# Attention placed by estimated due times, weight sums moved earlier, and a staggered last down product in a fused attention and maxout kernel

## Chip, cores and metric

The kernel runs on one core of one Trainium2 chip. The metric is the device time of one execution in microseconds (us): 328.72 us is the median of the three runs of the kernel before (327.97 the lowest).

## What is computed

The reference is attention followed by a feed-forward part that takes the largest of three up products:

```python
# q, k, v: batch 8, heads 12, tokens 448, head size 64
scores = scale * q @ k.T
m = max(scores); e = exp(scores - m)
attn = e / (sum(e) + exp(-m) + 1e-09)      # "softmax off by one"
x = (attn @ v), heads side by side         # 3584 tokens x 768
h = maximum(maximum(x @ w1, x @ w2), x @ w3)   # w1, w2, w3: 768 x 768
out = h @ w_out                            # 768 x 768, float32 out
```

## The kernel before

**Units of work.** Four heads of one batch make a group; there are 24 groups, three to a batch. A group's attention is cut into: seven score tiles ("U", `visit`, L306), each four matmuls on 64x64 quarters of TensorE into a pair of PSUM banks, followed by one `exp` on ScalarE (L317, 128x896); six sums of the exponentials on VectorE (`sum_e`, L327); the denominator ("D", `den_group`, L349: four matmuls with ones, then a logarithm on ScalarE, L362); its reciprocal as exp of minus that logarithm (`recip_group`, L369); and the product with v ("N", `num_group`, L373: 28 matmuls), whose two banks VectorE multiplies by the reciprocal into `xT` (`norm_group`, L397, two instructions). The feed-forward part is cut into pieces of 24 matmuls on 64x64 quarters (L789): an up piece (`up_piece`, evicted at L518, L520 or L523) or a down piece (`out_piece`, evicted at L567 or L575 and stored by `store`, L590).

**Three stages.** Up to about 74 us the first groups run with full 128x128 pieces (L534, L557). From there to 264 us every group's attention is laid among the pieces. The feed-forward part of the last two batches is done behind it, from 264 us on, with seven products in place of eight on half-size blocks (`up_unit` for the three up weights, `out_unit` for the down weight). This needs sums of weight blocks (`combine_weight`, L898, tiles `comb`), of x blocks (`combine_moving`, L907, tiles `sx`) and of h blocks (`sh`).

**What orders the middle stage.** The schedule is written out when the program is built; on the chip every engine runs its list in that order. `step` (L830) emits one step, a quarter-array matmul pair for each half of the rows, counted in `steps[0]`; a step stands for about 0.19 us of TensorE. `ORDER` (L858) is the order of a group, U U D U U N U U U, with the share of the group's steps that follow each part (`steps_for`). U, D and N take two pairs of PSUM banks in turn (`double`, L85), so that each one waits for what reads the banks of the one before the last: an exp, the logarithm, or the two norm multiplies. Work that must come some steps later is put in `late` by `after(n, ...)` and emitted by `do_late` (L801): the sums after 9, 14, 20 or 9 steps, and the two norm multiplies one and two steps after N. `given` holds, in steps, until when VectorE and ScalarE are booked; `give` and `first_free` add costs to it, and `first_free` uses it to choose the engine that evicts a piece.

**The last stage.** `in_turn` (L1134) emits the seven products of three units, product by product; a unit keeps two PSUM banks, "a" and "s", from a ring of eight (`tps`, L966, one pool with one tag, of which the first two turns are skipped). `put` (L1004) evicts a product's result; for weights 2 and 3 it goes to a buffer `c`, and `largest` (L1012) takes the maximum of all of `c` into `hp`, the tile `hT` of the last two batches, in one instruction of 1792 elements to a unit. `later(i)` puts the four sums for weight i+1 into slots 2 to 5 of weight i. After weight 3 the two held down tiles run (`plain`, L1107), then the four h sums, then the three units of `out_unit`: d[0] and d[1] side by side, d[2] mixed with the last plain tile at the end (L1153 to L1161). The output tiles of the units, `o1` and `o2`, come from the pool that the plain tiles use too (`out_pool`, five buffers). `ENDS` (L1056) gives the queues of the two stores of a tile: SP and SP, but POOL and POOL for `o2` of units 1 and 2.

Of the kernel before, what the change touches and what calls it, by code (L numbers as in the profile page):

```python
# [22 lines left out]
def kernel(  # L23
# [165 lines left out]

    steps = [0]  # L190
    given = {"dve": 0.0, "act": 0.0}

    def give(engine, cost):
        given[engine] = max(given[engine], steps[0]) + cost

    def first_free(dve_cost, act_cost):
        end = {e: max(given[e], steps[0]) + c for e, c in (("dve", dve_cost), ("act", act_cost))}
        e = "act" if end["act"] < end["dve"] else "dve"
        given[e] = end[e]
        return e  # L200

    def copy_qk(i, n):
        give("dve", 2.1)
# [102 lines left out]
    def visit(units):  # L306
# [8 lines left out]
        for st, j, stp in stps:  # L315
            give("act", 4.9)
            nc.scalar.activation(  # L317
                out=st["eT"][:, j], in_=stp[:, :, 0:S], func=AF.Exp, scale=scale, bias=-math.log(EDIV)
            )
        return mm  # L320

    def sum_e(i, j):
        give("dve", 3.3)
        st = state[i]
        if j == 1:
# [23 lines left out]
    def den_group(i):  # L349
# [10 lines left out]
        given["act"] = max(given["act"], given["dve"] + 2)  # L360
        give("act", 4.9)
# [4 lines left out]
    def recip_group(i):  # L366
        give("act", 5.1)
        st = state[i]
        nc.scalar.activation(  # L369
# [24 lines left out]
    def norm_group(i, banks, r):  # L394
        give("dve", 3.3)
# [108 lines left out]
    def up_piece(b, fc, i, bank=None, done=False):  # L504
# [12 lines left out]
        if i == 0 and done and first_free(3.3, 2.9) == "act":  # L517
# [3 lines left out]
        else:  # L521
            give("dve", 3.3)
# [28 lines left out]
    def out_piece(bp, t, nh, bank=None, done=False):  # L551
# [14 lines left out]
        if last or not done or first_free(2.9, 2.6) == "dve":  # L566
# [233 lines left out]

    def do_late(all_of=None):  # L801
        now = [x for x in late if x[0] <= steps[0] or x[1] is all_of]
        late[:] = [x for x in late if x not in now]
        for t, f, a in now:
            f(*a)
# [24 lines left out]
    def step():  # L830
        if count[0] == NDC * len(turns[0]) and (len(pieces) >= 3 or last_batch[0] and pieces):
# [4 lines left out]
            for r in range(2):  # L836
                turns[r] += [m + x for x in ((0, 2, 1), (1, 0, 2))[r] if x < len(now)]
        idle = not ready(0)
# [5 lines left out]
        do_late()  # L844

    def after(n, f, *a):
        late.append((steps[0] + n, f, a))

    debt = [0.0]

# [41 lines left out]
    def combine_weight(i, n):  # L892
        give("dve", 4.5)
# [19 lines left out]
    given.update(dve=0.0, act=0.0)  # L913
    batch_done(1)
    after(9, sum_e, MID, 1)
# [4 lines left out]
    for i in range(MID, NI + 1):  # L920
        for op, j, w in ORDER if i > MID else ORDER[4:]:
            if op == "U" and i < NI:
                mm = visit([(i, j)])
# [6 lines left out]
                if i == NI - 2 and j in (1, 3, 4, 6):  # L930
                    after(4, combine_weight, 0, (1, 3, 4, 6).index(j))
                if i == NI - 1 and j == 5:
                    after(4, lambda: combine_moving(sx, 2, *x_blocks()))
                if j > 0:
                    after({1: 9, 2: 14, 3: 20, 4: 9, 5: 9, 6: 9}[j], sum_e, i, j)
# [4 lines left out]
            if op == "D":  # L940
                if i == NI:
                    steps_for(12)
                do_late(sum_e)
                den_group(i - 1)
# [3 lines left out]
            if op == "N":  # L948
                pair = num_group(i - 1)
                steps[0] += 7  # L950
                for r in range(2):
                    after(1 + r, norm_group, i - 1, pair, r)
                b, g = groups[i - 1]
                if g == NG - 1:
                    after(10, batch_done, b)
            steps_for(rate[0] * w / TOTAL if i < NI else (8 if op == "D" else 0))
    while late or left() or count[1] < count[0]:
        step()

# [6 lines left out]
    tps = ctx.enter_context(tc.tile_pool(name="tps", bufs=8, space=bass.MemoryType.PSUM))  # L966
    for i in range(1, 4):
        comb[i] = tail.tile([128, 4, 3, DFF // 2], MMDT, name=f"comb{i}")
    for _ in range(2):
        tps.tile([128, 512], FP32, tag="tbank", name="first_two")  # L970
# [24 lines left out]
    def bank_of(u, which):  # L995
        u[which] = tps.tile([128, 512], FP32, tag="tbank", name="bank_" + which)

    def up_unit(i, f):
# [5 lines left out]
        def put(b, side, bank, other=None):  # L1004
# [4 lines left out]
            else:  # L1009
                nc.vector.tensor_tensor(out=dst, in0=other, in1=bank, op=ALU.add)  # L1010

        def largest():  # L1012
            if i > 0:
# [179 lines left out]
```

## Time and profile before

| | before |
|---|---|
| median of the runs | 328.72 us |
| the profiled execution, its own time | 329.01 us |
| its span, first to last instruction | 327.2 us |
| PE busy in the span | 304.5 us (93%) |
| DVE / ACT / POOL busy | 233.4 / 230.1 / 99.7 us |
| middle stage, first L789 matmul to last | 74.0 to about 263.3 us |
| first matmul of the last stage | 264.12 us |
| last matmul ends | 316.5 us |
| last work of DVE and ACT ends | 318.7 and 319.3 us |

Busy time says little here on PE: matmuls overlap (one of 448 columns is shown as 349 ns long, while four on different quarters start within 0.19 us), and a short pause of their starts can hide under the last one's end. So the holes are read from the starts in the timeline: where a run of L789 matmuls, which start about 0.05 us apart, is followed by a start that is late by more than that. The time outside the span is 1.8 us.

### The profile page before, as it was taken

To read this page: it belongs to the slowest core of one execution; us is meant where nothing else is said; L and a number is where in the kernel's file an instruction comes from. 1 tells how busy PE (TensorE), PEld (TensorE's weight loads), DVE (VectorE), ACT (ScalarE), POOL (GpSimd) and SP (SyncE) were. 2 spreads that over 40 slices of the span, in tenths; PEclk is the share of its full clock that TensorE was granted. 3 is DMA by queue.
4 is the path that set the end of the run, shared out by engine and by line. 5 is a ranking of instruction groups with operands and counts; after the bars stand their busy time and mean duration, and the time that the engine had idled before them with its cause. 6 is when DMAs were issued, how large, how long until landed. Compare 5 with 4: busy or idle time off the path is not lost.

```text
span 327.2 us, 12698 instructions
## 1 busy us (share of the span) xinstructions
PE 304.5 (93%) x5599; PEld 231.6 (71%) x5599; DVE 233.4 (71%) x426; ACT 230.1 (70%) x310; POOL 99.7 (30%) x171
## 2 busy tenths in 40 slices
PE   7679999999999999999999999899999999999960
PEld 6557777657777777889978899588976755555630
DVE  3437598997787777777868678788898475798720
ACT  2599859987776788788867897689777555464520
POOL 8767666640333233232323333232000000000020
PEclk9799999999999999999999999999999999999995
DMA  7999999999699997799977999969400150000365
GB/s 141 143 177 191 199 207 194 150 177 158 80 95 117 171 168 120 117 133 209 121 115 112 191 197 126 120 82 240 77 2 4 50 148 0 0 2 0 96 194 144
DMA packets 59352, 40.64 MB, mean 124 GB/s; under 512 B 32705, under 2 KB 55953, under 8 KB 59297
## 3 DMA queue, kind: packets, MB, share of 16 engines
q0 software_dynamic: 25584, 21.90, 47.8%
q1 hardware_dynamic: 33408, 17.50, 26.8%
q8 instruction: 44, 0.72, 0.9%
q10 hardware_dynamic: 304, 0.43, 0.5%
q14 instruction: 12, 0.09, 0.1%
HBM read 42.47 MB, written 11.01 MB: 163 GB/s over the span
## 4 chain that ended last, share of the span: by engine, by line
PE 77%; ACT 7%; issue 5%; DVE 5%; DMA 2%; POOL 2%; POOLq 0%; DVEq 0%
PE piece L789 37%; PE stp L293 8%; PE av L341 8%; PE bank_a L985 7%; PE bank_s L985 5%; PE p_i L534 4%; ACT eTp L416 3%; ACT eT L317 2%; PE piece L534 2%; DMA ld_q<-in_q_dram 2%; PE den L341 2%; DVE eS L327 2%; DVE hT L523 1%; DVE xT L397 1%; PE piece L557 1%
## 5 line engine op out<-in xcount | busy, mean ns | idle before, releaser
L317 ACT ACTIVATE eT<-stp 128x896 f16<-128x896 f32 x147 | 132.2, 917 | 40.7 <-PE stp L293 39.5
L789 PE MATMUL piece<-xT,w 64*64 64x448 f16 x2160 | 135.0, 349 | 0.5 <-DVE xT L397 0.3
L789 PEld LDWEIGHTS <-w 64*64 64x64 f16 x2160 | 90.0, 107 | 17.9 <-issue 2.0
L293 PE MATMUL stp<-qkT 64*64 64x448 f16 (+2 forms) x756 | 66.8, 334 | 3.3 <-DVE xT L397 1.0
L327 DVE TENSOR_TENSOR eS<-eS,eT 128x896 f16<-128x896 f16 x105 | 65.0, 619 | 3.7 <-ACT eT L317 1.1
L789 PE MATMUL piece<-w,hT 64*64 64x384 f16 x792 | 50.0, 323 | 0.3 <-DVE hT L523 0.2
L523 DVE TENSOR_TENSOR hT<-hT,piece 128x448 f16<-128x448 f16 x60 | 37.1, 619 | 18.4 <-PE piece L789 15.5
L112 POOL DMA_DIRECT2D ld_q<-in_q_dram x48 | 28.8, 606 | 53.2 <-PE stp L293 25.4
L112 POOL DMA_DIRECT2D ld_v<-in_v_dram x48 | 28.5, 599 | 46.9 <-PE stp L293 25.5
L789 PEld LDWEIGHTS <-hT 64*64 64x64 f16 x792 | 34.8, 107 | 4.8 <-issue 0.8
L293 PEld LDWEIGHTS <-qkT 64*64 64x64 f16 x756 | 28.5, 107 | 12.4 <-issue 6.7
L112 POOL DMA_DIRECT2D ld_k<-in_k_dram x46 | 27.9, 612 | 23.4 <-PE piece L789 10.6
L341 PE MATMUL av<-eT,ld_v 64*64 64x448 f16 x588 | 32.7, 349 | 0.0
L397 DVE TENSOR_TENSOR xT<-av,rb 128x448 f16<-128x448 f32 x42 | 24.2, 618 | 10.5 <-PE av L341 10.2
L341 PEld LDWEIGHTS <-ld_v 64*64 64x64 f16 x756 | 27.0, 108 | 5.4 <-issue 0.2
L590 POOL DMA_DIRECT2D out_dram<-o_sb x5 | 2.7, 538 | 91.6 <-DVE o_sb L1073 86.2
L416 ACT ACTIVATE eTp<-stp 128x768 f16<-128x768 f32 (+3 forms) x24 | 18.1, 821 | 9.4 <-PE stp L293 9.3
L534 PEld LDWEIGHTS <-w 128*128 128x128 f16 x216 | 18.9, 98 | 5.2 <-issue 3.9
L362 ACT ACTIVATE rb<-den 128x896 f32<-128x896 f32 x21 | 19.3, 918 | 3.9 <-PE den L341 3.3
L369 ACT ACTIVATE rb<-rb 128x896 f32<-128x896 f32 x21 | 20.0, 953 | 0.2
L567 DVE TENSOR_SCALAR o_sb<-piece 128x384 f32<-128x384 f32 x22 | 12.0, 554 | 9.1 <-PE piece L789 8.8
L985 PEld LDWEIGHTS <-comb 128*128 128x128 f16 x108 | 10.6, 98 | 9.9
(102 smaller groups left out, 335.1 us busy)
## 6 DMA issues: line engine op xcount, KB each, us to landing
out_dram<-o_sb SPq DMA_DIRECT2D x50, 192.0 KB, 4.0
ld_q<-in_q_dram POOLq DMA_DIRECT2D x48, 112.0 KB, 4.4
ld_v<-in_v_dram POOLq DMA_DIRECT2D x48, 112.0 KB, 4.1
ld_k<-in_k_dram POOLq DMA_DIRECT2D x46, 112.0 KB, 4.1
w<-in_moe_w_dram POOLq DMA_DIRECT2D x6, 192.0 KB, 6.7
w<-in_moe_w_out_dram POOLq DMA_DIRECT2D x3, 384.0 KB, 8.4
w<-in_moe_w_dram POOLq DMA_DIRECT2D x2, 384.0 KB, 6.2
out_dram<-o_sb POOLq DMA_DIRECT2D x4, 192.0 KB, 4.6
```

The lines of the kernel that those rows point to most:

```text
L112: return eng.dma_start(out=dst[hp * KC : hp * KC + KC].rearrange("p s j d -> p s (j d)"), in_=src[:, half_heads(name, hp)],)
L293: mm = nc.tensor.matmul(out=out[half(c), r], lhsT=qkT[half(r), 0, j, h], rhs=qkT[half(r), 1, q0:q1, h], start=True, stop=True,)
L317: nc.scalar.activation(out=st["eT"][:, j], in_=stp[:, :, 0:S], func=AF.Exp, scale=scale, bias=-math.log(EDIV))
L327: nc.vector.tensor_tensor(out=st["eS"], in0=st["eT"][:, 0] if j == 1 else st["eS"], in1=st["eT"][:, j], op=ALU.add,)
L341: nc.tensor.matmul(out=outs[r][half(c)], lhsT=weights(r, c), rhs=moving(r, c), start=start, stop=stop,)
L369: nc.scalar.activation(out=st["rb"], in_=st["rb"], func=AF.Exp, bias=math.log(LAMBDA), scale=-1.0)
L397: nc.vector.tensor_tensor(out=xT[b][:, 2 * g + r, :], in0=banks[r][:, 0:S], in1=state[i]["rb"][:, r], op=ALU.mult)
L416: nc.scalar.activation(out=eT[:, j0 : j0 + n].rearrange("p j r q -> p r j q"), in_=stp[:, :, 0 : n * nq].rearrange("p r (j q) -> p r j q", ...
L523: nc.vector.tensor_tensor(out=dst, in0=dst, in1=p_i[:, 0:S], op=ALU.max)
L534: nc.tensor.matmul(out=p_i[:, ts(j, nq)], lhsT=w_sb[i][:, dc, ts(2 * fp + j, 128)], rhs=xT[b][:, dc, q0 * KC : q1 * KC], start=(dc == 0), ...
L789: nc.tensor.matmul(out=p["bank"][half(c), 0:w], lhsT=lhs(k, r, c), rhs=rhs(k, r), start=(r == p["first"] and k == 0), stop=(r != p["first" ...
L985: nc.tensor.matmul(out=bank, lhsT=lhs(k), rhs=rhs(k), start=start and k == 0, stop=k == 2, skip_group_check=True,)
```

## The change

The kernel's first stage stays. In the middle stage:

- Costs in `given` are lowered (exp 4.9 to 4.2 steps, sums 3.3 to 2.8, and so on); `give` becomes `book`, which takes the time at which the data is ready and returns the booked end plus `SEEN` (1 step).
- `pair_free` keeps, for each pair of banks, the step at which it is estimated to be free. `for_pair` emits piece steps until then ahead of every U, D and N; those steps are taken off what `steps_for` emits later.
- A sum is due at the estimated end of its exp. D comes when its sums are booked as done. The two norm multiplies are emitted together (`norm_both`), due at the booked end of the reciprocal or one step after N.
- The four sums of weight 1 and the x sum `sx[2]` are no longer tied to units of the last two groups but lie in `spare`, from which `do_late` takes one whenever VectorE is booked as free; so weight 1's sums come at the start of the stage.

In the last stage:

- The eight banks come from four pools of 2, 4, 1 and 1 banks, used in the order 4, 2, 1, 1.
- The sums of weights 2 to 4 are moved forward by the table `LATER`: all of weight 2's and 3's lie in weight 1's slots (two in each of the last three), all of weight 4's in weight 2's, none in weight 3's.
- For weight 3, the maximum is taken by each `put` at once (448 elements each), and the last product's bank goes straight into the maximum on VectorE, in place of a ScalarE copy and one maximum of 1792 elements.
- `o1` and `o2` have buffers of their own, three each. Every store of the units goes half to SP, half to POOL.
- The h sums come after the first of the two held tiles; the second one's halves are used between the units' products; the three units are staggered instead of side by side.

```diff
+    def book(engine, cost, ready=0.0):
+        given[engine] = max(given[engine], ready, steps[0]) + cost
+        return given[engine] + SEEN
...
+            st["e", j] = pair_free[turn[0] % 2] = book("act", 4.2, steps[0] + 2)
...
+        st["sum"] = book("dve", 2.8, st["e", j])
...
+        pair_free[turn[0] % 2] = book("act", 4.3, steps[0] + 2)
...
+        if spare and given["dve"] <= steps[0]:
+            f, a = spare.pop(0)
             f(*a)
...
+    def steps_until(when):
+        while steps[0] < when():
+            debt[0] -= 1
+            if not step():
+                break
+    def next_pair():
+        return pair_free[(turn[0] + 1) % 2]
+    def for_pair(also=0.0):
+        steps_until(lambda: max(next_pair(), also))
+        if any(x[1] is norm_both and x[2][2] == (turn[0] + 1) % 2 for x in late):
+            do_late(norm_both)
...
+    def norm_both(i, pair, n):
+        for r in range(2):
+            norm_group(i, pair, r)
+        pair_free[n] = given["dve"] + SEEN
...
+        if i == NI - 2:
+            spare.append((combine_moving, (sx, 2, *x_blocks())))
...
+    spare += [(combine_weight, (0, n)) for n in range(4)]
...
             if op == "U" and i < NI:
+                for_pair()
                 mm = visit([(i, j)])
...
-                    after({1: 9, 2: 14, 3: 20, 4: 9, 5: 9, 6: 9}[j], sum_e, i, j)
+                    at(state[i]["e", j], sum_e, i, j)
...
             if op == "D":
-                if i == NI:
-                    steps_for(12)
+                steps_until(lambda: steps[0] + 1 if any(x[1] is sum_e for x in late) else 0)
                 do_late(sum_e)
+                for_pair(state[i - 1]["sum"])
                 den_group(i - 1)
...
             if op == "N":
+                for_pair()
                 pair = num_group(i - 1)
...
-                for r in range(2):
-                    after(1 + r, norm_group, i - 1, pair, r)
+                t = max(steps[0] + 1, state[i - 1]["recip"])
+                pair_free[n] = max(t, given["dve"]) + 5.6 + SEEN
+                at(t, norm_both, i - 1, pair, n)
...
-    tps = ctx.enter_context(tc.tile_pool(name="tps", bufs=8, space=bass.MemoryType.PSUM))
+    tps = [
+        ctx.enter_context(tc.tile_pool(name=f"tps{n}", bufs=n, space=bass.MemoryType.PSUM))
+        for n in (2, 4, 1, 1)
+    ]
+    tps = [tps[1]] * 4 + [tps[0]] * 2 + [tps[2], tps[3]]
...
-    for _ in range(2):
-        tps.tile([128, 512], FP32, tag="tbank", name="first_two")
...
+            if i == 2:
+                h = hp[:, f + 3 * side, b * S : b * S + S]
+                nc.vector.tensor_tensor(out=h, in0=h, in1=dst, op=ALU.max)
...
-            if i > 0:
+            if i == 1:
                 dst = hp[:, f:NFC:3]
                 nc.vector.tensor_tensor(out=dst, in0=dst, in1=u["c"], op=ALU.max)
...
-            put(0, 1, bank)
+            if i == 2:
+                dst = hp[:, f + 3, 0:S]
+                nc.vector.tensor_tensor(out=dst, in0=dst, in1=bank, op=ALU.max)
+            else:
+                put(0, 1, bank)
...
-    ENDS = ((SY, SY), (SY, SY)), ((GP, GP), (SY, SY)), ((GP, GP), (SY, SY))
+    ENDS = [[(nc.sync, nc.gpsimd)] * 2] * 3
...
-            u["o1"] = out_pool.tile([128, DM], FP32, tag="o_sb", name="o_sb")
+            u["o1"] = tail.tile([128, DM], FP32, tag="o1", name="o1", bufs=3)
...
+    LATER = (
+        ((), (), ((1, 0),), ((1, 1),), ((1, 2), (2, 0)), ((1, 3), (2, 1)), ((2, 2), (2, 3))),
+        ((), ((3, 0),), ((3, 1),), ((3, 2),), ((3, 3),)),
+        (),
+    )
...
-    for m in range(3):
-        d[m][0]()
-        d[m][1]()
-    for slot in range(2, 6):
-        for m in range(2):
-            d[m][slot]()
     e = plain(B // 2 - 1, NT - 1, 0) + plain(B // 2 - 1, NT - 1, 1)
-    for x in (d[0][6], d[2][2], d[1][6], d[2][3], e[0], d[2][4], e[1], d[2][5], e[2], d[2][6], e[3]):
+    for x in (
+        *fill[:4], h_sum[0], h_sum[1], d[0][0], d[0][1], h_sum[2], d[1][0], d[1][1],
+        h_sum[3], d[2][0], d[0][2], fill[4], d[1][2], fill[5], d[0][3], d[2][1], d[0][4], d[1][3], d[0][5], d[1][4],
+        d[0][6], d[2][2], d[1][5], d[2][3], d[1][6], fill[6], d[2][4], fill[7], d[2][5], e[0],
+        d[2][6], e[1], e[2], e[3],
+    ):
         x()
```

## The prediction, made before the changed kernel was run

> **What bounds the kernel now.** I read the page's busy lines first, then the waits of PE, then timelines of PE at each hole, and at last the timeline of the end. The page:
>
> ```profile
> PE 304.5 (93%) x5599; PEld 231.6 (71%) x5599; DVE 233.4 (71%) x426; ACT 230.1 (70%) x310; POOL 99.7 (30%) x171
> ...
> PEclk9799999999999999999999999999999999999995
> DMA  7999999999699997799977999969400150000365
> ```
>
> PE is the bound: 93% busy at the full clock, while no other engine is over 71%. The change leaves PE's work as it is (both programs issue the same 5599 matmuls), so it can only give or take three things: holes in PE's stream, the 10.7 us between the last matmul's end (316.5) and the span's end (327.2), and new waits. The first stage, up to 74 us, is not touched. The waits of PE:
>
> ```profile
> PE stp L293 <- DVE xT L397: 1.0, 3, 0.4
> ...
> PE bank_a L985 <- DVE o_sb L567: 0.7, 1, 0.7
> ...
> PE den L341 <- DVE eS L327: 0.4, 1, 0.4
> ```
>
> These are small because a matmul's shown end covers part of a hole. The timeline shows the holes whole (start, length, then what ran):
>
> ```profile
> 203.73 1.00 PE L789 MATMUL piece<-xT,w 64*64 64x448 f16 x16
> ...
> 204.45 0.62 DVE L327 TENSOR_TENSOR eS<-eS,eT 128x896 f16<-128x896 f16 x1
> 204.99 0.62 DVE L327 TENSOR_TENSOR eS<-eT 128x896 f16<-128x896 f16 x1
> ...
> 205.12 0.38 PE L341 MATMUL den<-eS,ones 64*64 64x448 f16 x4 [0.40 <-DVE eS L327]
> ```
>
> The last of the 16 matmuls starts at 204.37, D's first at 205.12; the step is 0.05, so 0.70 us are lost, because D was issued while the last sum of its group still ran. Counted this way, 76 to 262 us has thirteen holes of 0.2 us or more: at D 106.81 (0.29), 173.02 (0.24), 205.12 (0.70), 245.84 (0.50); at the U that waits for the norm multiplies 145.93 (0.62), 168.20 (0.54, and 0.33 behind it), 211.81 (0.74); at pieces 104.12 (0.40), 113.09 (0.41), 180.97 (0.22), 237.69 (0.30), 255.85 (0.49). Together 5.8 us. A fourteenth stands before the last stage, 0.94 us at 264.12. The end:
>
> ```profile
> 315.38 0.65 PE L985 MATMUL bank_a<-w,sh 128*128 128x384 f16 x3 [0.23 <-DVE o_sb L1073]
> ...
> 317.36 0.56 DVE L567 TENSOR_SCALAR o_sb<-bank_a 128x384 f32<-128x384 f32 x1 [2.03 <-DMA out_dram<-o_sb]
> 317.83 0.55 DVE L1073 SCALAR_TENSOR_TENSOR o_sb<-bank_s,u 128x384 f32<-128x384 f32 x1
> ...
> 318.30 0.35 DVE L567 TENSOR_SCALAR o_sb<-bank_a 128x192 f32<-128x192 f32 x1
> ```
>
> VectorE stands still for 2.03 us, for a buffer whose store has not landed; two evictions queue behind it. DMA's share by stretches of 2 us (columns: stretch, length, busy us of PE, PEld, DVE, ACT, POOL, clock, DMA share, GB/s):
>
> ```profile
> 312.00:314.00 2.00, 2.00 (x14) 1.18 (x13) 0.00 (x0) 1.25 (x3) 0.77 (x2) 1.00 0.99 255
> 314.00:316.00 2.00, 1.77 (x12) 0.97 (x10) 0.56 (x1) 0.00 (x0) 0.00 (x0) 1.00 0.92 308
> 316.00:318.00 2.00, 0.52 (x4) 0.10 (x1) 0.65 (x2) 0.00 (x0) 0.00 (x0) 1.00 0.63 227
> 318.00:320.00 2.00, 0.00 (x0) 0.00 (x0) 0.64 (x2) 0.71 (x2) 1.56 (x3) 1.00 0.36 103
> ```
>
> The stores come in one burst from 311 us, starve while VectorE waits, and come again.
>
> **The change part by part.** I go by the order of both programs' instructions and count the PE work that lies between the matmuls a wait depends on and the instruction that waits.
>
> *Placement, term A.* (1) D: between the scores two visits back and D lay 1.75 to 2.27 us of work, now 2.13 to 2.59, and D is held back until the sums are booked as done. The four holes at D (1.73) should go. (2) Norm multiplies: before, sums stood between and ahead of them (at 145.93, three VectorE instructions of 0.62 us that waited for the same matmuls or older ones); now the two stand together with one older one ahead, and the next use of their banks keeps its distance (2.02 us against 1.94). Needed: 0.17 to start, 1.15 for the two, 0.06 to wake PE, so 1.4. These holes (2.23) should go. (3) Pieces: at 113.09 the order is the same, 0.41 stays; at 255.85 the x sum of 0.86 us still stands ahead, 0.49 stays; of 180.97 I keep 0.1; the two others lose a sum of 0.62 us ahead, or gain 0.2 us of distance, and go. Kept: 1.0. (4) New: with D later, the U that takes D's banks has only 1.16 to 1.51 us behind it (before 1.38 to 1.89), and the logarithm needs 0.17 + 0.92 + 0.06 = 1.15. Where ScalarE is free this is just enough; behind an exp it costs some 0.15, and five groups stand under 1.25: 0.7. One maximum now stands behind both norms (0.36), the last D has 1.30 us where it had 1.46 (0.2), and a little for what I don't see (0.3): 1.6. So A = -5.8 + 1.0 + 1.6 = -3.2. Ends: -4.8 if nothing new comes; 0 if each of the 16 groups pays 0.2 at the logarithm.
>
> *Sums in `spare`, no term.* The same five sums; the four of 0.75 us now stand at the start of the stage, the x sum of 0.86 us where it was. VectorE has 141 of 186 us to do there. If one lands ahead of a maximum it costs 0.75 once; that lies in A's ends.
>
> *Banks of the last stage, term B.* One pool of eight made the first product wait for the eviction of the very last piece. In the new order the first four banks are those of N, read 5.35 us of work before, and the x sums follow the norms directly, no longer behind that eviction. The 0.94 goes: B = -0.9. The next candidate, the third product that waits for the first sum's eviction, has 1.13 us for 0.17 + 0.62 + 0.06, so nothing is late. End: -0.3, if the x sums start no earlier.
>
> *Weight sums forward, no term.* Two more sums of 0.75 in each of three slots of weight 1; VectorE stood still there from 269.9 to 271.8 and from 276.5 to 278.6. The sum evictions of weight 2 end at about 281.2, the fourth product that needs them starts at 281.2 to 282.3 for the three units, and each finds its own done 1 us before. If that cover went, up to 0.75.
>
> *Maximum in quarters, term C.* For weight 3 VectorE does, per unit, three of 448 elements and one from PSUM, for one of 1.08. The rows 0.62 (896) and 1.08 (1792) put 448 at 0.39. An eviction and its maximum depend on each other: 0.62 + 0.39 = 1.01. From the fifth product's first matmuls: six pairs 6.06, three PSUM maxima at a pitch of 0.56 make 1.7, start and wake-up 0.23, in all 8.0 us. PE reaches d[0]'s second product after 7.3 us of work, since the cover is now one held tile (1.95 us) in place of two. So PE waits 0.7: a new wait. Ends 0 and 1.2 (if a short maximum takes as long as an eviction's pitch, 0.54, and every pair 1.1). The hole of 0.23 at 315.38 goes. C = +0.7 - 0.2 = +0.5.
>
> Here the Trainium skill speaks against the change: VectorE: DVE Perf Modes, section on the TRN2 errata, says that every VectorE instruction pays a fixed extra time, so that tiles should have at least 512 elements. The direction agrees with the rows above (four times 448 costs 1.8 us, one of 1792 costs 1.08). By the page's 58 + FD/2 cycles at 0.96 GHz a short maximum is 0.29 us, an estimate, the chain 7.4 us, and C would be -0.1; I go by the rows.
>
> *The end, term D.* Let T be the last matmul's end. Before, the last eviction ended at T + 2.2, held by the 2.03. With own buffers it ends at T + 0.7 (start 0.2, ScalarE's 0.33 behind one DMA issue). Then: the last SP store, 4.5 us from issue to landing (its row); 2.5 from the last landing (about 324.7) to the span's end, in which POOL drains its queue; 0.3 for SP's line. T + 8.0 against T + 10.7: D = -2.7. Check by DMA: the eight tiles stored here have 3.15 MB, at 300 GB/s 10.5 us from about T - 5.3: landed at T + 5.2, plus 2.5. So it is close to the DMA's own limit, and the ends are -3.5 and +0.4 (227 GB/s: 13.9 us).
>
> The Trainium skill, DMA: Bandwidth & Descriptors, section on the issuing engine by pattern, gives plain stores to Sync and calls the GpSimd path the slower one; the rows agree in direction (landing 4.2 us from SP, 4.6 from POOL). By its first-byte figures POOL's stores would be 0.4 later, an estimate.
>
> **Sum.** -3.2 - 0.9 + 0.5 - 2.7 = -6.3 us on the profiled execution's 329.01 (span 327.2 and 1.8 around it): 322.7. The median of the runs is 0.3 below that execution, so 322.5, 1.9% faster.
>
> **Rivals.** (a) *Placement only moves the holes*: A = 0, 325.7. For: the distance at the logarithm shrinks in every group. Against: the holes had plain causes in the order, and those causes are gone. (b) *The end stays*: stores at 227 GB/s, or POOL's drain lasting longer with seven DMAs for five, D = +0.4: 325.6. For: DMA is 0.99 busy at 312 us. Against: it idles at 318. (c) *The logarithm becomes the wait in every group, and it ends slower*: with an exp ahead (pitch 0.8) the logarithm ends 1.95 us behind D, against 1.32: 0.63 in each of 16 groups, +10.1 for the 1.6 I set, about 331. It decides from 0.5 us a group on. Against: in most groups the exp ahead depends on scores that end about 1.3 us before D starts, so with 0.17 + 0.92 it is done. (d) *All goes well*: A -4.8, C -0.2, D -3.5: 319.4.
>
> **How the numbers follow.** Forecast 0.55 (320.5 to 324.5), (a) 0.14, (b) 0.14, (c) 0.05, (d) 0.12. The range 319.4 to 326.2 leaves out (c) and some of (d) and of (a) with (b) together. A measurement of this kernel can tell about 2% from no change; 2% faster is 322.15, just under my number. Faster by more: all of (d) and half of the forecast, 0.40; slower by more: (c), 0.04; the rest 0.56.
>
> **What would show it.** A: no hole over 0.2 us at D or at the U behind the norms; the logarithm named as releaser of U would be my 1.6 or rival (c). B: the first matmul of the last stage starts without a wait. C: PE waits for the maximum (the new line behind `put`) once, about 0.7 us, soon after the first held tile. D: no DMA among VectorE's releasers at the end, DMA busy without a gap, and the span ending about 8 us after the last matmul. Wrong would be: the DMA still moving 7 us after the last matmul, or POOL as the last engine with a drain that grew.

## The result, and the profile after

The changed kernel took 323.65 us (median of 4 runs, 322.99 to 325.11), beside 328.03 us for the kernel before (327.97 to 328.72): a ratio of 0.9866, interval 0.9822 to 0.9911. One slow run of the kernel before, of 634.25 us, is left out here; the 328.72 us given ahead of the prediction is a median that counts it. The changed kernel is 1.3% faster, inside the range, and within the 2% that a measurement is taken to tell here. Measured once more, with 12 runs (e11 below), the ratio was 0.9915 (0.9885 to 0.9945). The profiled execution took 322.99 us, its span 321.2.

The changed kernel's page:

```profile
PE 302.7 (94%) x5599; PEld 233.3 (73%) x5599; DVE 233.7 (73%) x431; ACT 230.9 (72%) x311; POOL 100.5 (31%) x173
...
DMA  7999999999589997889986999779300250000185
```

PE is still the bound and has the same 5599 matmuls. The last three DMA slices, of 8 us each, are 1, 8 and 5 tenths busy, for 3, 6 and 5 before: the last burst of stores is more in one piece. Of the waits of PE, those in the middle stage:

```profile
PE piece L792 <- DVE hT L526: 0.4, 1, 0.4
PE piece L792 <- DVE xT L400: 0.3, 1, 0.3
```

The three lines shown of before (the scores behind the norm multiply, the last stage's first bank, D behind its sum) have no counterpart: they are gone. In the middle stage these two lines at pieces are what is left. The place that answers to before's hole at 205.12, in the timeline:

```profile
202.13 0.62 DVE L331 TENSOR_TENSOR eS<-eT 128x896 f16<-128x896 f16 x1
202.20 0.44 PE L345 MATMUL den<-eS,ones 64*64 64x448 f16 x4
...
202.39 0.44 PE L297 MATMUL stp<-qkT 64*64 64x448 f16 x4
...
202.58 1.39 PE L792 MATMUL piece<-xT,w 64*64 64x448 f16 x24
```

D (`den`) starts at 202.20, 0.19 us before the scores, which start 0.19 before the pieces: the stream is unbroken. The sum at 202.13 belongs to the next group. The largest hole that the change made is here:

```profile
245.99 1.16 DVE L400 TENSOR_TENSOR xT<-av,rb 128x448 f16<-128x448 f32 x2 [1.09 <-PE piece L792]
...
247.06 0.62 DVE L331 TENSOR_TENSOR eS<-eS,eT 128x896 f16<-128x896 f16 x1
...
247.60 1.15 DVE L526 TENSOR_TENSOR hT<-hT,piece 128x448 f16<-128x448 f16 x2
248.26 0.35 PE L792 MATMUL piece<-w,hT 64*64 64x384 f16 x2 [0.38 <-DVE hT L526]
```

Two norm multiplies (`xT`) and a sum (`eS`) run one after the other on VectorE, and the maximum (`hT`) that the next piece needs stands behind all three: PE loses 0.68 us. The end, by its timeline, and then DMA by stretches (columns as in the prediction):

```profile
311.01 0.56 DVE L570 TENSOR_SCALAR o_sb<-bank_a 128x384 f32<-128x384 f32 x1 [0.91 <-DMA out_dram<-o]
...
311.30 0.65 PE L1180 MATMUL bank_a<-w,hT 128*128 128x384 f16 x3
...
311.66 3.33 SPq L593 DMA_DIRECT2D out_dram<-o  x2
...
312.38 0.33 ACT L582 ACTIVATE o_sb<-bank_a 128x192 f32<-128x192 f32 x1 [1.36 <-DVE o_sb L570]
...
315.09 1.61 SPq L593 DMA_DIRECT2D out_dram<-o_sb  x1
```

```profile
308.00:310.00 2.00, 2.00 (x15) 1.17 (x12) 1.01 (x2) 0.58 (x2) 0.53 (x2) 1.00 0.97 314
...
312.00:314.00 2.00, 0.00 (x0) 0.00 (x0) 0.34 (x1) 0.33 (x1) 0.39 (x1) 1.00 1.01 297
314.00:316.00 2.00, 0.00 (x0) 0.00 (x0) 0.00 (x0) 0.00 (x0) 0.00 (x0) 0.97 0.93 216
316.00:318.00 2.00, 0.00 (x0) 0.00 (x0) 0.00 (x0) 0.00 (x0) 0.00 (x0) 0.50 0.84 281
318.00:320.00 2.00, 0.00 (x0) 0.00 (x0) 0.00 (x0) 0.00 (x0) 0.00 (x0) 0.50 0.05 16
```

The last eviction ends at 312.71, 0.76 us behind the last matmul (T = 311.95). The label "DMA" on VectorE's 0.91 misleads: the matmul that this eviction reads ends at 310.97, 0.04 before it, so the wait was for PE. The stores now run without a gap from 306.38 to 318.47. SP's queue, which issues two stores in 1.17 us at 111.28, takes 1.4 to 1.9 us for each of its last three here, and the last one goes out only at 315.09, T + 3.1.

**Where the 6.0 us of span came from.** I cut each span at the first matmul of the middle stage, the first of the last stage and T:

| us | before | after | difference |
|---|---|---|---|
| first stage | 73.95 | 72.36 | -1.59 |
| middle stage | 190.17 | 187.11 | -3.06 |
| last stage up to T | 52.40 | 52.48 | +0.08 |
| T to the span's end | 10.71 | 9.26 | -1.45 |

The first stage's 1.59 us are not the change's: no edit touches it. In before, a load comes late and the granted clock falls behind the wait (timeline, then a stretch):

```profile
11.35 0.58 PE L219 MATMUL trT<-ident,ld_q 128*64 128x128 f16 x14 [1.88 <-DMA ld_q<-in_q_dram]
...
13.99 0.96 PE L219 MATMUL trT<-ident,ld_q 128*64 128x128 f16 x14
```

```profile
14.00:16.00 2.00, 2.00 (x46) 1.83 (x46) 1.64 (x3) 1.11 (x2) 2.00 (x4) 0.50 0.99 122
```

Clock is the third number from the end, 0.50, and fourteen transposes take 0.96 us for 0.58. The changed kernel waited 0.67 us at that place, and has 1.00 in every stretch from 10 to 18 us. e4 and e5 (below), whose first stage is the changed kernel's, show the same fall and took 73.0 and 73.7 us for it. The other three stages together, the change itself, are worth -4.43 us in the profile.

### The profile page after: what moved, and what is told of

Read it like the earlier page. It is cut to its first block, busy times and chain, and to the rows that moved or that the text cites. A ratio compares the mean times of both kernels' runs of the same rounds, so it can differ in the third digit from the quotient of the medians.

```text
span 321.2 us, 12696 instructions
## 1 busy us (share of the span) xinstructions
PE 302.7 (94%) x5599; PEld 233.3 (73%) x5599; DVE 233.7 (73%) x431; ACT 230.9 (72%) x311; POOL 100.5 (31%) x173
## 4 chain that ended last, share of the span: by engine, by line
PE 80%; ACT 5%; DMA 4%; DVE 3%; POOL 3%; issue 2%; ACTq 0%; DVEq 0%; POOLq 0%
PE piece L792 42%; PE stp L297 8%; PE av L345 8%; PE bank_a L1035 7%; PE bank_s L1035 5%; PE p_i L537 4%; DMA w<-in_moe_w_dram 3%; PE piece L537 2%; ACT eT L321 2%; DMA ld_q<-in_q_dram 2%; PE den L345 2%; DVE c L1061 1%; PE piece L560 1%; POOL ld_v L112 1%; ACT eTp L419 1%
## 5 line engine op out<-in xcount | busy, mean ns | idle before, releaser
L792 PEld LDWEIGHTS <-w 64*64 64x64 f16 x2160 | 93.5, 107 | 16.5 <-issue 2.8
L297 PE MATMUL stp<-qkT 64*64 64x448 f16 (+2 forms) x756 | 68.4, 332 | 2.6 <-ACT eTp L419 0.8
L792 PE MATMUL piece<-w,hT 64*64 64x384 f16 x792 | 48.6, 323 | 0.4 <-DVE hT L526 0.4
L297 PEld LDWEIGHTS <-qkT 64*64 64x64 f16 x756 | 30.3, 106 | 11.4 <-issue 5.7
L593 POOL DMA_DIRECT2D out_dram<-o x6 | 3.2, 536 | 87.1 <-DVE o L1130 86.3
L537 PE MATMUL p_i<-xT,w 128*128 128x192 f16 (+1 forms) x156 | 16.5, 257 | 1.4 <-DMA w<-in_moe_w_dram 0.9
```

The source lines that it names most:

```text
L297: mm = nc.tensor.matmul(out=out[half(c), r], lhsT=qkT[half(r), 0, j, h], rhs=qkT[half(r), 1, q0:q1, h], start=True, stop=True,)
L537: nc.tensor.matmul(out=p_i[:, ts(j, nq)], lhsT=w_sb[i][:, dc, ts(2 * fp + j, 128)], rhs=xT[b][:, dc, q0 * KC : q1 * KC], start=(dc == 0), ...
L792: nc.tensor.matmul(out=p["bank"][half(c), 0:w], lhsT=lhs(k, r, c), rhs=rhs(k, r), start=(r == p["first"] and k == 0), stop=(r != p["first" ...
```

## The experiments

One table for all. The stages are as above; the end of the last DMA packet (its landing is signalled some 0.3 us later) and the span's end are given behind T. "Stages" is the difference to before in middle, last stage and end together. "Timed" is the ratio of the runs with its interval, and that times 327.5 us as a difference; four kernels ran once only.

| run | middle | last | DMA ends | span ends | stages | timed |
|---|---|---|---|---|---|---|
| before | 190.17 | 52.40 | +7.95 | +10.71 | | |
| after | 187.11 | 52.48 | +6.52 | +9.26 | -4.4 | 0.9866 (0.9822-0.9911), -4.4 |
| e1 middle only | 187.80 | 52.00 | +8.38 | +11.18 | -2.3 | 0.9957 (0.9929-0.9984), -1.4 |
| e2 last only | 189.43 | 52.87 | +6.34 | +9.12 | -1.9 | 0.9978 (0.9957-0.9998), -0.7 |
| e3 no POOL stores | 187.47 | 52.48 | +6.89 | +8.38 | -5.0 | 0.9831 (0.9805-0.9857), -5.5 |
| e4 tiles first | 189.41 | 52.22 | +5.86 | +9.27 | -2.4 | 0.9876 (0.9821-0.9931), -4.1 |
| e5 tiles first, no POOL | 187.11 | 52.22 | +6.45 | +7.94 | -6.0 | 0.9820 (0.9787-0.9853), -5.9 |
| e6 tiles first, early POOL | 187.11 | 52.22 | +5.60 | +6.85 | -7.1 | 0.9787 (0.9761-0.9813), -7.0 |
| e7 norms apart | 188.40 | 52.47 | +6.51 | +9.33 | -3.1 | one run |
| e8 D unheld | 186.42 | 52.47 | +6.51 | +9.37 | -5.0 | one run |
| e9 one maximum | 187.66 | 52.54 | +6.41 | +9.45 | -3.6 | one run |
| e10 own buffers | 190.13 | 52.01 | +6.78 | +9.59 | -1.6 | one run |
| e11 changed, again | 187.19 | 52.48 | +6.47 | +8.96 | -4.7 | 0.9915 (0.9885-0.9945), -2.8 |
| e12 combined | 188.25 | 52.21 | +5.71 | +6.97 | -5.9 | 0.9777 (0.9751-0.9803), -7.3 |

### e1 and e2: either half alone

e1 is the changed kernel up to the end of the middle stage with before's last stage behind it; e2 is the reverse.

> The middle stage of the changed kernel (placement by estimates, sums in `spare`) with the last stage of the kernel before. Theory (the holes at D and at the U behind the norm multiplies were real losses and the placement removes them): the stretch from the first L789 matmul to the first matmul of the last stage falls from 190.2 us by 2 to 3 us, the hole of about 0.9 us ahead of the last stage stays, time about 2.5 us under the kernel before. Rival (placement only moves the holes, the gain of the change lies at its end): the stretch stays within 0.7 us of 190.2 and the time within 0.7 us of the kernel before.

> The middle stage of the kernel before with the last stage of the changed kernel (banks from four pools, sums forward, maximum in quarters, own buffers, staggered order, stores half SP half POOL). Theory: 0.7 us from the banks and about 1.4 us from the end (span's end 9.2 us behind the last matmul, where it was 10.7), a wait of 0.5 us for the maximum: 1.5 to 2.2 us under the kernel before. Rival (all of the gain lies here): 4 us or more under it.

e1's middle stage took 187.80: placement alone gave -2.37. Its end came at T + 11.18, 0.5 later than before's. e2's middle stage took 189.43, -0.74, which is the banks, and its end was T + 9.12. So neither half holds the whole gain. The stages came out as expected; the times did not, with 1.4 us gained where 2.5 was expected of e1, and 0.7 where 1.5 to 2.2 was expected of e2. e2's last stage was 0.47 longer than before's: a new hole of 0.39 stands 3.81 us into it, where the third product waits for the first sum's eviction. That is the wait whose cover (1.13 us for 0.85) term B named; with before's order of the middle stage the x sums come behind the last piece's eviction again, and the cover is gone.

### e3: no POOL stores at the end

In the changed kernel POOL's last store lands at 317.23, but POOL's closing drain ends at 320.42 and SP's own last wait at 319.14; the span ends 0.75 to 0.79 behind the later of the two in every run. These ends of engines were read from the trace's records.

```
-    ENDS = [[(nc.sync, nc.gpsimd)] * 2] * 3
+    ENDS = [[(nc.sync, nc.sync)] * 2] * 3
```

and the other store on GpSimd, half of the last tile, moved to SP as well.

> The changed kernel with every store of the last product on SP and ACT, none on POOL. Theory (the end is bound by the DMA engines, about 3.15 MB at 268 GB/s, whichever queue issues): SP has twelve stores of the units to issue at 0.6 to 1 us each, the last landing moves by less than 1 us to either side, but POOL's closing drain, which ended 1.3 us behind SP's last wait, could end earlier: -1.3 to +1 us against the changed kernel. Rival 1 (POOL's packets, shown as 0.2 to 0.3 us each against 0.1, take the DMA engines' time): DMA done 2 us or more earlier and a time 2 us lower. Rival 2 (SP's line is the bound): last SP issue 2 us or more later, time 2 us or more higher.

The DMA ended 0.37 us later (T + 6.89), the span 0.88 sooner (T + 8.38): POOL's drain, not the last landing, set the changed kernel's end. Stretches of e3:

```profile
316.00:318.00 2.00, 0.00 (x0) 0.00 (x0) 0.00 (x0) 0.00 (x0) 0.00 (x0) 0.50 0.90 237
318.00:320.00 2.00, 0.00 (x0) 0.00 (x0) 0.00 (x0) 0.00 (x0) 0.00 (x0) 0.50 0.22 58
```

The DMA share is still 0.22 in the last two microseconds, where the changed kernel had 0.05; and the span ends sooner.

### e4, e5, e6: the last stage's stores earlier

e4 puts all eight parts of the two held tiles (`fill`) ahead of the h sums, none of them between the units' products, so that the second tile is stored sooner and the first wait of term C has more cover:

```
-        *fill[:4], h_sum[0], h_sum[1], d[0][0], d[0][1], h_sum[2], d[1][0], d[1][1],
-        h_sum[3], d[2][0], d[0][2], fill[4], d[1][2], fill[5], d[0][3], ...
+        *fill, h_sum[0], h_sum[1], d[0][0], d[0][1], h_sum[2], d[1][0], d[1][1],
+        h_sum[3], d[2][0], d[0][2], d[1][2], d[0][3], ...
```

e5 is e4 with e3's edit. e6 is e4 with POOL storing only the second halves of the first two units; unit 2 and the last tile go to SP and ACT:

```
+    ENDS = [[(nc.sync, nc.gpsimd)] * 2] * 2 + [[(nc.sync, nc.sync)] * 2]
```

> The changed kernel with both held tiles ahead of the h sums and the units, in place of the second one's halves spread between the units. Theory: the cover for the maxima is 3.9 us again in place of 1.95, so the wait of 0.47 us behind the first held tile goes; the second held tile's 0.39 MB is stored about 8 us earlier, when the DMA engines stand still, so that the burst at the end is shorter by up to 1.4 us, of which 1 us is lost since the first unit's stores come two half tiles later; no new wait over 0.3 us between the units. In all 0.5 to 1.5 us under the changed kernel. Rival (the halves are needed as cover between the units' products): PE waits between the units of 0.5 us or more, and a time equal to the changed kernel's or above it.

> The changed kernel with both held tiles ahead of the units and all stores of the last product on SP and ACT. Theory (the span ends by the later of two: SP's last wait plus 1.5 us, about 0.3 us behind the last landing, or POOL's closing drain, which ends 3.1 us behind POOL's own last landing, plus 0.75): without POOL's stores the end is the last landing plus 1.8; the DMA ends about 6 us behind the last matmul because one tile less is in the burst; the span ends 7.5 to 8 us behind the last matmul (changed kernel 9.3), the last stage takes 52.2 us, time about 1.7 us under the changed kernel, near 321.5. Rival (what ended the span was only the drain, and the burst is not shortened by the tile stored early): 8.4 us behind the last matmul as without POOL's stores alone.

> As the kernel with tiles first and no POOL stores, but POOL keeps its halves of the stores of units 0 and 1, which land first; unit 2 and the last tile go to SP and ACT. Theory: POOL's last landing is at least 3 us ahead of the last one, so its drain is over in time, and SP has fewer stores to issue in line: the span ends 7.3 to 7.8 us behind the last matmul, 0 to 0.3 us better than without POOL's stores. Rival (the drain starts only when every DMA is done, or when POOL has issued anything in this stage): the span ends 1.3 us later, 8.8 or more behind the last matmul.

In e4 the wait behind the maxima halved (0.42 to 0.21, last stage 52.22) and the DMA ended 0.66 us sooner, but the span's end stayed (T + 9.27): POOL's last store landed at 319.94, its drain ended at 323.13, 3.19 us later. e5 ended at T + 7.94. There the DMA ended at 6.45, 0.6 later than with POOL's help in e4. SP's own waits in e5, from 304 us on, hold a line that those of the changed kernel, e4 and e6 do not have:

```profile
SPq L593 <- DMA out_dram<-o_sb: 1.8, 2, 1.2
```

Twice, for 1.2 us up to 316.02 and 0.6 us up to 317.73, SP issued nothing until an earlier store had landed; e3, with as many stores on SP, has such waits too. So SP's line held e5's last stores back. e6 has both: POOL's last landing at 312.78 and its drain over at 315.85, ahead of the last landing, and T + 6.85, better than forecast. (By time e5 and e6, 0.9820 and 0.9787, can't be told apart; the 1.1 us is that of their profiles.) DMA in e6, at the start of the burst and at the end (T = 310.83):

```profile
300.00:302.00 2.00, 2.00 (x14) 1.21 (x13) 2.00 (x4) 1.38 (x3) 0.00 (x0) 1.00 0.76 197
...
314.00:316.00 2.00, 0.00 (x0) 0.00 (x0) 0.00 (x0) 0.00 (x0) 0.00 (x0) 0.95 0.85 267
316.00:318.00 2.00, 0.00 (x0) 0.00 (x0) 0.00 (x0) 0.00 (x0) 0.00 (x0) 0.50 0.10 29
```

The second held tile's stores run here at 300.3 to 302.0; in the changed kernel no byte moves from 300.75 to 306.38. The last burst is shorter by as much: 2.77 MB for 3.16.

e4's middle stage is not slower by its order: it has one PE pause of 1.89 us in front of the piece at 203.52, to which the profile gives no other releaser than "issue" (the last section has more on it); 187.5 without it.

### e7: norm multiplies apart again

```
-                at(t, norm_both, i - 1, pair, n)
+                for r in range(2):
+                    after(1 + r, norm_group, i - 1, pair, r)
...
```

The lines left out make the two other calls of `norm_both` (for the last x sum and the end of a batch) by themselves.

> The changed kernel with the two norm multiplies emitted one and two steps after N as before, so that other VectorE work can stand ahead of and between them; all else as changed. Theory (that work made the holes at the U behind N): holes of 0.2 to 0.8 us come back at four or more of these places, and the middle stage is 1.5 to 2.5 us longer than the changed kernel's 187.1. Rival (the holes went because for_pair holds U back): the middle stage within 0.5 us of 187.1.

The holes at the U behind the norms came back: four with 0.53, 0.74, 0.48 and 0.47 us, another 0.47 at the pieces behind the first of them, and two smaller ones of 0.27 and 0.28. The middle stage was 1.3 longer than the changed kernel's 187.11: less than expected, but by the step named. The line of PE's waits, and one of the places:

```profile
PE stp L297 <- DVE xT L400: 1.1, 4, 0.4
```

```profile
207.04 0.62 DVE L331 TENSOR_TENSOR eS<-eS,eT 128x896 f16<-128x896 f16 x1
207.57 0.62 DVE L400 TENSOR_TENSOR xT<-av,rb 128x448 f16<-128x448 f32 x1
...
208.25 0.38 PE L297 MATMUL stp<-qkT 64*64 64x448 f16 x4 [0.44 <-DVE xT L400]
```

A sum stands between the two norm multiplies and delays the second; the scores (`stp`) wait for it. The waits line of before is back.

### e8: D not held back

```
             if op == "D":
+                if i == NI:
+                    steps_until(...)
                 do_late(sum_e)
-                for_pair(state[i - 1]["sum"])
+                if i == NI:
+                    for_pair(state[i - 1]["sum"])
```

> The changed kernel with D issued at its old place in the step count: it neither waits for the sums to be booked as done nor for its banks. Theory (D was issued ahead of its last sum): holes of 0.2 to 0.7 us come back at some of the 17 D, the middle stage is 0.7 to 1.7 us longer than 187.1. Rival (the earlier due times of the sums alone made D's holes go): within 0.4 us of 187.1.

The theory fell. The delays at D came to 0.44 us (0.31 without this edit, 1.70 before), with one new hole over 0.2, of 0.24 at 211.39, and the middle stage became 0.7 us shorter (186.42). D stood again 1.7 to 2.2 us of work behind the scores two visits back, as before; in the changed kernel it is 2.1 to 2.6 in most groups. So neither holding D nor that distance removed the holes. What is left of the change there is that each sum is due when its exponential is booked as done, and no longer a fixed number of steps after its scores, beside what the norms and `for_pair` at U and N move on VectorE; that the due times alone are enough was not tried. Holding D cost at the pieces: the changed kernel's hole of 0.68 is gone, and delays at pieces fell from 2.79 to 1.98, though two holes of 0.60 and 0.43 (164.47, 196.73) are new. The same place in e8:

```profile
245.21 1.15 DVE L400 TENSOR_TENSOR xT<-av,rb 128x448 f16<-128x448 f32 x2
...
246.28 0.61 DVE L526 TENSOR_TENSOR hT<-hT,piece 128x448 f16<-128x448 f16 x1
...
246.81 0.62 DVE L331 TENSOR_TENSOR eS<-eS,eT 128x896 f16<-128x896 f16 x1
```

The maximum comes straight behind the norms, the sum after it.

### e9: maximum of weight 3 in one instruction

Both branches `if i == 2:` off, `largest` back for weight 3.

> The changed kernel with the maximum of weight 3 taken as before, one instruction of 1792 elements to a unit behind the last product, which goes to the buffer by ScalarE. Theory (VectorE's line sets when the units may start): the three maxima start when the last product's copies end and take 3.1 us behind the last product, against 1.95 us of cover, so PE waits 1.3 to 1.8 us behind the first held tile in place of 0.47, and the last stage takes 53.3 to 53.8 us. Rival (four instructions cost more than one, cutting gained nothing): a wait of 0.5 us or less.

The expectation fell: the last stage took 52.54 against 52.48. PE's wait is 0.52 at one place, for two waits of 0.21 with the quarters. Each unit's maximum of 1.08 us waits only for its own copies:

```profile
295.87 3.09 DVE L1069 TENSOR_TENSOR hT<-hT,c 128x1792 f16<-128x1792 f16 x3 [0.52 <-ACT c L1059]
```

The first could start at 295.87, while evictions went on, so the chain that is left at the end is hardly longer. Cutting into quarters gained 0.06 us.

### e10: own output buffers alone

Before with one edit, `u["o1"] = tail.tile([128, DM], FP32, tag="o1", name="o1", bufs=3)`, and the same for `o2`.

> The kernel before with one edit: `o1` and `o2` of the last product have buffers of their own. Theory (the evictions at the end waited 2 us for a buffer, and the DMA engines starved meanwhile): no DMA among VectorE's releasers at the end, the last eviction ends 0.5 to 0.8 us behind the last matmul (2.2 before), and the span ends 1.2 to 2 us sooner behind it than 10.7. Rival (the DMA engines set the end, the wait was hidden behind them): less than 0.7 us sooner.

```profile
316.18 0.36 DVE L567 TENSOR_SCALAR o_sb<-bank_a 128x192 f32<-128x192 f32 x1 [0.88 <-PE bank_a L1123]
```

The last eviction waits for PE and no longer for a store's landing: the end went from 10.71 to 9.59 (1.1 sooner, for 1.2 to 2 expected), and the last stage from 52.40 to 52.01. These two make 1.5 us, as much as the changed kernel gets in both stretches with the stagger, the queues and the quarters together (1.4): beside the buffers, these added nothing in sum.

### e11 and e12: the changed kernel again, and the best one

> The changed kernel as it is, for its time on the same chip. Expected 1.2 to 1.4% under the kernel before; the middle stage 187.1 us, the last stage 52.5 us and the end 9.3 us again, within 0.2 us each, while the first stage moves by up to 2 us with the clock that is granted there.

e11's stages repeat those of the changed kernel to 0.1 us, 0.3 at the end. Its timed gain of 0.85% was under what was expected of it.

e12 joins e6 and e8.

> The kernel with tiles first and POOL's stores for units 0 and 1 only, and in addition D issued at its old place in the step count, not held back. Theory (from the run with D not held: holding D costs 0.7 us net, since the sums' earlier due times alone keep them ahead of D; the end is independent of the middle stage): middle stage 186.4 us, last stage 52.2, span's end 6.8 to 7.0 us behind the last matmul; about 0.7 us under the same kernel with D held, near 320.1, which is 2.2 to 2.4% under the kernel before. Rival (the 0.7 us was one execution's chance): middle stage 187.0 or more, no gain over it.

It took 320.17 us against 327.15: 0.9777 (0.9751 to 0.9803), whole interval below those of the changed kernel. It beats both kernels, with an end at T + 6.97. Its middle stage holds another pause of 1.79 us (at 119.04) put down to "issue", and is 186.46 without it: the 0.7 us of e8 came again. From e6 (0.9787) it can't be told apart.

## Why the prediction was right or wrong

The number, 322.5 us, was 1.15 us (0.4%) below the measured 323.65, the side "within 2%" was the likeliest named, and PE's stream and the end were the right two places. But that is in part luck. The agreement of the profiled execution (322.99, forecast 322.7) owes 1.6 us to the first stage, which no edit touches; the change's own sum was -4.4, not -6.3. By time the gain was 4.4 us in the first measurement and 2.8 in the second (e11), for 6.2 forecast. And the 0.3 us from the execution to the median rests on a median that counts the run of 634.25 us. By its steps, delays of PE's stream being counted as in the prediction:

| step | forecast | measured |
|---|---|---|
| A(1) holes at D, with the last D | -1.73 + 0.2 | -1.39 |
| A(2)+(4) U: norms, logarithm | -2.23 + 0.7 | -1.2 |
| A(3)+(4) pieces, with one maximum and what was not seen | 1.82 to 1.0, + 0.36 + 0.3 | 2.54 to 2.79, so +0.25 |
| A in all | -3.2 | -2.34 |
| B banks | -0.9 | -0.72 |
| C in all | +0.5 | +0.08 |
| D the end | -2.7 | -1.45 (e11: -1.75) |

(The delay totals count small holes too, so before's stand at 6.9 against the 5.8 + 0.94 counted from 0.2 us up. How a delay is shared between a hole at D or U and the pieces beside it depends on the counting, by some 0.3 us; the sum of A and B, -3.06, does not.)

**A.** The forecast was 0.9 too good. Part of that is the reading of the holes: matmuls start four at a time, a four every 0.19 us, so the D at 205.12 was due at 204.49 and lost 0.63 us, not 0.70, and the short holes are overstated by as much. Counted by what the stream never makes up (the smallest lag of any later start behind that pitch), the thirteen holes come to 4.3 us and not 5.8. The other part lies at the pieces. Of the 1.0 kept there only the hole of 0.41 is left, but five new ones of 0.24 to 0.68 (137.85, 165.05, 166.12, 238.13 and 248.26) make 1.7 us, for 0.36 and 0.3 allowed. The largest, 0.68 behind the norms and a sum, is gone both with D not held (e8) and with the norms apart (e7). The logarithm was over-priced: 0.7 for five groups, while eight small delays at U come to 0.33, of which the logarithm's part is some 0.2. Rival (c) is out. The norms' step is confirmed by e7. For D the result was right, with a hole of 0.31 left at the last D where 0.2 was priced, and the reason wrong (e8): neither the distance nor the holding was needed.

**B.** Right in mechanism: the first matmul of the last stage starts 0.20 late, for 0.94 before, and e2 shows -0.74 for it alone.

**C.** The chain was as priced, a pair of eviction and maximum at 0.95 for 1.01 us and a short maximum at 0.39 as worked out:

```profile
290.96 0.62 DVE L1061 TENSOR_TENSOR c<-p,bank_a 128x448 f16<-128x448 f32 x1 [2.02 <-ACT p L1073]
291.62 0.39 DVE L1064 TENSOR_TENSOR hT<-hT,c 128x448 f16<-128x448 f16 x1
```

The wait came where it was forecast, behind the first held tile, 0.42 us in two parts for 0.7, and the hole at the end, by e10's last stage, gave 0.39 for 0.2. The estimate of 0.29 us from the Trainium skill's 58 cycles, by which nothing would have waited, falls. The same section (VectorE: DVE Perf Modes, the TRN2 errata) adds that the 58 is too low and that some 150 cycles were measured; (150 + 224) / 0.96 GHz is 0.39 us, an estimate, which the row agrees with. The prediction had taken the table without the note behind it. What the prediction did not see is that the cut itself is worth 0.06 (e9).

**D.** This is the step that failed most: T + 8.0 forecast, T + 9.26 measured. By its terms:

| term of D, us | forecast | measured |
|---|---|---|
| last eviction ends, behind T | 0.7 | 0.76 |
| until the last SP store is issued | 0.3 | 2.38 |
| its issue to its landing | 4.5 | 3.72 |
| last landing to the span's end | 2.5 | 2.40 |

The term that failed is SP's line: the last store went out at T + 3.14, behind issues of 1.4 and 1.9 us, while the burst moved 3.16 MB in 12.1 us, 262 GB/s against the 300 assumed. Whether the full DMA engines stretched SP's issues, or the issues held the engines, no run separates. So the last landing came at T + 6.86 for T + 5.5. The last term has the right size by chance. It is not a constant: it is 0.92 in e6, 1.15 in e3 and 3.06 in e4. POOL's drain ends 3.07 to 3.20 us behind POOL's own last landing in every run that stores by POOL at the end, so what counts is when POOL's last store lands. I named the drain in rival (b), but as one that grows with the number of DMAs. It grew by less than 0.1: 3.11 us before with five stores on POOL in the last 20 us, 3.19 after with seven. The Trainium skill (DMA: Bandwidth & Descriptors, the issuing engine by pattern) gives plain stores to Sync; e3 agrees, with 0.9 us, while e6 shows that early stores on POOL still help.

**What stays open.** The sums over the stages and the timed gains agree within 0.6 us for after, e3, e5 and e6 but e1, e2 and e11 gained 0.9 to 1.9 us less by time than by stages, and e4 and e12, with a pause in the profiled execution, 1.4 to 1.7 more. Single pauses and the first stage make single profiled executions differ by about that much; it was not settled whether they make up all of it.

## What to carry to other kernels

Ask at the end of a kernel which engine's last instruction ends the span, and not only when the last byte lands: an engine with a fixed closing time (POOL's drain here) should get the early stores, and the last ones go to a queue without it. When a sum is moved away from one wait, look at the instruction that now stands behind it; here, holding one step back until its inputs were ready cost more at its neighbours than it saved. Compare two profiled executions stage by stage, and leave out a stage that the change does not touch before calling a sum confirmed.

## What the runs showed of the hardware

POOL's drain, from the trace's records (last landing of a POOL store, end of the drain, difference in us):

| run | landing | drain ends | difference |
|---|---|---|---|
| before | 323.34 | 326.45 | 3.11 |
| after | 317.23 | 320.42 | 3.19 |
| e4 | 319.94 | 323.13 | 3.19 |
| e6 | 312.78 | 315.85 | 3.07 |
| e10 | 321.83 | 324.94 | 3.11 |

In e3 and e5, where POOL stores nothing at the end, its drain ends 2.91 us behind the landing of its last load (225.65 and 226.68), long before the span's end.

The clock of the first stage, over the fourteen profiled executions, goes with how long PE stood before the transposes of `ld_q` at about 10 us, mostly for that load. With waits of 1.66 to 2.05 us (before, e1, e5, e10) the granted clock then fell to 0.5 for 3.41 us; with 0.44 to 0.67 (after, e3, e6, e7, e8, e9) it did not; with 0.92 to 1.25 it did twice (e4, e12) and twice not (e2, e11). The trace's clock records settle what decides there. In each profile the granted clock keeps one value for whole multiples of 3.41 us (6.83, 3.41, then 300 to 311), but for the last value, which the end of the profile shortens. Divide each profile into windows of 3.41 us from its first clock record on. In the second window, in which that wait ends, PE is busy (by matmul ends as the profile models them) for 25, 26, 30, 39, 40 and 44% of the time in before, e1, e10, e5, e12 and e4, and the clock is 0.5 in the window behind it. In the eight others PE is busy for 49 to 77%, and the clock stays at 1.00. So the busy share of a fixed window goes with the fall, and where the wait lies in its window counts too: e2 and e11 waited longer (1.18 and 1.25 us) than e4 and e12 (0.92) and kept the clock. The middle stage began at 72.6 to 74.0 us with the fall (73.5 on average), at 71.5 to 73.1 without (72.3). The Trainium skill (TensorE: Matmul & The Clock Gate, section on what is actually happening) says that the clock is granted by PE's recent activity, judged over free-running windows of about 3.4 us: these records agree, with 3.41 us.

Two profiles hold one pause of PE in the middle stage, of 1.89 us in e4 and 1.79 us in e12, that is put down to "issue", as in e4:

```profile
203.52 0.38 PE L792 MATMUL piece<-xT,w 64*64 64x448 f16 x2 [1.59 <-issue]
```

No work or clock change is visible behind it, but a transfer is: the DMA records hold loads of instructions on queue q8, one at 200.84 to 202.20 ahead of this pause (the queue's line for 200.80 to 202.30 us: packets, MB, share):

```profile
q8 instruction: 1, 0.02, 5.7%
```

All eight idle times of PE over 0.2 us behind 10 us that the fourteen traces put down to "issue" (in after, e1, e3, e4, e8, e9 and two in e12) end 1.3 to 1.6 us behind the end of such a load. The load ahead of e4's pause came at 127.8 us from the start of the middle stage, where the five other runs with this middle stage and no such pause (after, e3, e5, e6, e11) have the same load at 122.4 to 123.2. So late instruction loads are the likely cause; no experiment here tries it.
